# P.V. of all sixteen key tiles accumulated in PSUM, with the next score fill ahead of it on TensorE

## The chip, the cores and the metric

The kernel runs on one core of one Trainium2 chip. A core has a matrix engine (TensorE, PE; its weight loads are shown as PEld), a vector engine (VectorE, DVE), an engine for activation functions (ScalarE, ACT), GpSimd (POOL) and SyncE (SP), which here only issues DMAs. The metric is the device time of one execution in microseconds; lower is better.

## The reference

Four layers run one after the other on x of 2048 rows by 512 columns: attention (A), gated MLP (B), A, B, each with a layernorm ahead and a residual sum behind. The attention has 32 heads of 16 columns that share one K and one V:

```python
q = (x @ wq).reshape(B, S, H, Dh).transpose(0, 2, 1, 3)     # S 2048, H 32, Dh 16
k = x @ wk
v = x @ wv
scores = jnp.einsum('bhqd,bkd->bhqk', q, k) * Dh ** (-0.5)
p = _softmax(scores, axis=-1)
o = jnp.einsum('bhqk,bkd->bhqd', p, v)
return o.transpose(0, 2, 1, 3).reshape(B, S, H * Dh) @ wo
```

Layer B is not touched by the change.

## The kernel before

The kernel writes one list of operations per engine; each engine works its list off in order, and semaphores join them (`K.op`, L53, adds one operation with its waits and its increment). So the order in which `layer_A` calls its helpers is the order on every queue.

**Tiling.** A layer has 4 query chunks (qc) of 512, in each 8 head groups (hg) of 4 heads, and in each of those 16 key tiles (kt) of 128. One triple is a *unit* (L504): 512 units per layer, and 32 *groups* of 16 units. A unit has four *blocks*, one for each head j: the scores of 128 keys by 512 queries, which fill one of PSUM's eight banks.

**Fill** (`emit_fill`, L734): three blocks at a time go into three of banks 0 to 5, each by one matmul that uses 32 rows of the array (L756). Fill i waits until exp i-2 has read those banks. Three blocks make one *iteration* i; there are 683 per layer.

**Exp** (`emit_exp`, L763): one ScalarE instruction reads three banks (128 x 1536) and writes bf16 into three of the twelve slots of `P_ring` (L775). The last one of a layer has two blocks.

**P.V.** (`emit_pv`, L780): four matmuls per unit, one for each head, each on 32 columns of the array, write o transposed into bank 6 (`pv_bank`, L795). A column of ones in `V_aug` gives the denominator of the softmax along with it. Three units fall into every four iterations: in one iteration of four there is none (`iu`, L519).

**Accumulation** (`emit_acc`, L800): DVE copies bank 6 into `acc_sb` at the first key tile (L816), adds bank 6 to it at the next fourteen (L818) and at the last one adds and writes bf16 into `oT_bf` (L820). The next P.V. waits for this read of bank 6 (semaphore `S_acc`, L789).

**Side tasks** (`emit_side_pe`, L535, and `emit_side_dve`, L568): everything else of the layer goes in small tasks, a TensorE part into bank 7 and a DVE part out of it. A task's TensorE part waits for the DVE part of the task before, since there is one side bank. Tasks are: K, V and the transposed x (at the start), the q projections (L489), the transposes of `w_sp` for layer B (L624, layer 0 only, with its DMAs, L611 and L645), at each group's end four transposes of `oT_bf` with a reciprocal and a normalising multiply (`make_fin_task`, L661 to L675), and at each chunk's end two transposing tasks and four projections by `wo` (L699, L717, L722). Urgent tasks may go in every iteration, the others in every second.

**The order of one iteration** (L838 to L846): exp i; P.V. and its accumulation of the units whose blocks are now all there; fill i+2; one side task's TensorE part; one side task's DVE part.

Of the kernel before, what the change touches and what calls it, by code (L numbers as in the profile page):

```python
# [5 lines left out]
FP32 = mybir.dt.float32  # L6
BF16 = mybir.dt.bfloat16
ACTF = mybir.ActivationFunctionType
ALU = mybir.AluOpType
# [95 lines left out]
def bass_interleave_layers__grouped_kv_mqa__mixer_gmlp__prompt_kernel(  # L105
# [16 lines left out]
    NT = S // 128  # L122
    QC = min(512, S)
    assert S % QC == 0
    NQC = S // QC
    NQT = QC // 128
# [4 lines left out]
    K = _B(nc)  # L131
    P = 128
# [16 lines left out]
    S_acc = K.sem()  # L149
# [32 lines left out]
    def pool_memset(ap, val, waits=()):  # L182
# [7 lines left out]
        waits=[(S_pool, v_id0)], inc=S_pool)  # L190
# [4 lines left out]
    with ExitStack() as wst:  # L195
# [23 lines left out]
        def dve_memset(ap, val, waits=()):  # L219
# [8 lines left out]
            waits=[(S_dve, v0), wA], inc=S_dve)  # L228
# [6 lines left out]
            waits=[(S_dve, v0), wA], inc=S_dve)  # L235
# [6 lines left out]
            waits=[(S_dve, v0), wA], inc=S_dve)  # L242
# [91 lines left out]
    def layer_A(layer_idx, x_waits, do_wspt=False):  # L334
# [6 lines left out]
        xn = K.sb([P, NT, D], BF16, lst, name="xnA")  # L341
        qT_pad = K.sb([P, 8, S], BF16, lst, name="qT_pad")
        P_ring = K.sb([P, 12, QC], BF16, lst, name="P_ring")
        acc_sb = K.sb([P, QC], FP32, lst, name="acc_sb")
        oT_bf = K.sb([P, 2, QC], BF16, lst, name="oT_bf")
        o_norm = K.sb([P, NQT, D], BF16, lst, name="o_norm")
        onT = K.sb([P, 2, 4, QC], BF16, lst, name="onT")
# [313 lines left out]
        def make_fin_task(qc, hg, par, acc_val):  # L661
            def pe_fn(e):
                ins = None
                for qt in range(NQT):
                    ins = e.transpose(side_bank16[:, qt * 128:(qt + 1) * 128], oT_bf[:, par, qt * 128:(qt + 1) * 128], ident[:])  # L665
                return ins

            def dve_recip(e):
                src = side_bank16[:, 0:NQT * 128].rearrange("p (qt j r) -> p qt j r", qt=NQT, j=4)[:, :, :, DH]
                return e.reciprocal(rden[:, 0:NQT, :], src)  # L670

            def dve_norm(e):
                src = side_bank16[:, 0:NQT * 128].rearrange("p (qt j r) -> p qt j r", qt=NQT, j=4)[:, :, :, 0:DH]
                dst = o_norm[:, 0:NQT, hg * 64:(hg + 1) * 64].rearrange("p qt (j d) -> p qt j d", d=DH)
                return e.tensor_tensor(dst, src, rden[:, 0:NQT, :, None].to_broadcast([P, NQT, 4, DH]), ALU.mult)  # L675

            task = {
                "pe": pe_fn,
                "pe_waits": [(S_acc, acc_val), (S_pool, v_ident)],
                "dve": [dve_recip, dve_norm],  # L680
                "dve_waits": [],
                "urgent": True,
            }

            def on_pe(v, par=par, grp=qc * 8 + hg):
                fin_pe_val[par] = v
                fin_pe_grp[par] = grp
            task["on_pe_emitted"] = on_pe
            return task

        def make_ont_task(qc, half, par):
            qts = [qt for qt in range(2 * half, min(2 * half + 2, NQT))]

            def pe_fn(e):
                ins = None
                for qi2, qt in enumerate(qts):
                    for c in range(4):
                        slot = qi2 * 4 + c
                        ins = e.transpose(side_bank16[:, slot * 128:(slot + 1) * 128],  # L699
                                          o_norm[:, qt, c * 128:(c + 1) * 128], ident[:])  # L700
                return ins

            def dve_fn(e):
                nq = len(qts)
                dst = onT[:, par, :, qts[0] * 128:(qts[0] + nq) * 128].rearrange("p c (qt q) -> p c qt q", q=128)
                src = side_bank16[:, 0:nq * 4 * 128].rearrange("p (qt c q) -> p c qt q", qt=nq, c=4)
                return e.tensor_copy(dst, src)

            return {"pe": pe_fn, "pe_waits": [(S_pool, v_ident)], "dve": [dve_fn], "dve_waits": [], "urgent": True}

        def make_wo_task(qc, qt, par):
            t = qc * NQT + qt

            def pe_fn(e):
                ins = None
                for c in range(4):
                    ins = e.matmul(side_bank32[:, 0:D], onT[:, par, c, qt * 128:(qt + 1) * 128], wo_r[:, c, :],  # L717
                                   start=(c == 0), stop=(c == 3))
                return ins

            def dve_fn(e):
                return e.tensor_tensor(X[:, t, :], side_bank32[:, 0:D], X[:, t, :], ALU.add)  # L722

            task = {"pe": pe_fn, "pe_waits": [wA], "dve": [dve_fn], "dve_waits": xw_for(x_waits, t), "urgent": True}

            def on_dve(v):
                x_done_vals.append(v)
            task["on_dve_emitted"] = on_dve
            return task
# [33 lines left out]
        def emit_exp(i):  # L763
            blocks = fill_blocks(i)
            n = len(blocks)
            b0 = 3 * (i % 2)
            s0 = (3 * i) % 12
            wl = [(S_fill, fill_base + i + 1)]
            if i >= 4:
                old_blocks = fill_blocks(i - 4)  # L770
                max_u = old_blocks[-1] // 4
                wl.append((S_pv, pv_base + max_u + 1))

            def act_fn(e, n=n, b0=b0, s0=s0):
                return e.activation(P_ring[:, s0:s0 + n, :],  # L775
                                    bank32(b0, n).rearrange("p (k q) -> p k q", k=n)[:, :, 0:QC],
                                    ACTF.Exp, scale=DH ** -0.5)
            K.op("act", act_fn, waits=wl, inc=S_exp)

        def emit_pv(u):  # L780
            qc, hg, kt = units[u]
            kc = kt // CT
            while kc not in V_ready:
                progressed = emit_side_pe()
                progressed = emit_side_dve() or progressed
                assert progressed, "V block task missing"
            wl = [(S_exp, exp_base + iu(u) + 1), V_ready[kc], prologue_done]
            if u >= 1:
                wl.append((S_acc, acc_base + u))  # L789

            def pe_fn(e):
                ins = None
                for j in range(4):
                    slot = (4 * u + j) % 12
                    ins = e.matmul(pv_bank[32 * j:32 * j + 32, 0:QC], V_aug[:, kt, 32 * j:32 * j + 32], P_ring[:, slot, :],  # L795
                                   tile_position=(0, 32 * j), start=True, stop=True)
                return ins
            K.op("pe", pe_fn, waits=wl, inc=S_pv)

        def emit_acc(u):  # L800
            qc, hg, kt = units[u]
            grp = u // NT
            par = grp % 2
            wl = [(S_pv, pv_base + u + 1)]
            if u >= 1:
                wl.append((S_acc, acc_base + u))
            last = (kt == NT - 1)
            if last and grp >= 2:
                while fin_pe_grp[par] != grp - 2:
                    assert emit_side_pe(allow_bg=False), "pending finalize missing"  # L810
                    emit_side_dve()
                wl.append((S_spe, fin_pe_val[par]))
            if NT == 1:
                fn = lambda e: e.tensor_copy(oT_bf[:, par, :], pv_bank[:, 0:QC])
            elif kt == 0:
                fn = lambda e: e.tensor_copy(acc_sb[:], pv_bank[:, 0:QC])  # L816
            elif not last:
                fn = lambda e: e.tensor_tensor(acc_sb[:], pv_bank[:, 0:QC], acc_sb[:], ALU.add)  # L818
            else:
                fn = lambda e: e.tensor_tensor(oT_bf[:, par, :], pv_bank[:, 0:QC], acc_sb[:], ALU.add)  # L820
            v = K.op("dve", fn, waits=wl, inc=S_acc)
            if last:
                side_urgent.append(make_fin_task(qc, hg, par, v))
                if hg == 7:
                    qpar = qc % 2
                    nhalf = (NQT + 1) // 2
                    for half in range(nhalf):
                        side_urgent.append(make_ont_task(qc, half, qpar))
                    for qt in range(NQT):
                        side_urgent.append(make_wo_task(qc, qt, qpar))  # L830

        pending_pv = {}
        for u in range(U):
# [3 lines left out]
            emit_fill(1)  # L837
        for i in range(NI):  # L838
            emit_exp(i)
            for u in pending_pv.get(i, []):  # L840
                emit_pv(u)
                emit_acc(u)
            if i + 2 < NI:
                emit_fill(i + 2)
            emit_side_pe(allow_bg=(i % SIDE_PERIOD == 0))
            emit_side_dve()  # L846
        for i in range(NI, NI + 8):
            for u in pending_pv.get(i, []):
                emit_pv(u)
                emit_acc(u)  # L850
        while side_pending() or side_state["k_dve"] < len(side_emitted):
            progressed = emit_side_pe()
            progressed = emit_side_dve() or progressed
# [258 lines left out]
    v = None  # L1112
# [36 lines left out]
```

## Time and profile before

| | us |
|---|---|
| median of 3 runs | 2634.82 (2631.36 to 2640.33) |
| span of the profiled execution | 2633.1 |
| TensorE busy (PE) | 1897.9 (72%) |
| VectorE busy | 1225.5 (47%) |
| ScalarE busy | 2066.9 (78%) |
| GpSimd busy | 43.9 (2%) |

The profile gives the profiled execution by its span, from the first instruction to the last; there is no other time for it. Busy is the time in which an engine had at least one instruction running; instructions of one engine can overlap, so the number of instructions times their mean duration can be more than the busy time. "Idle before" is the time without any instruction ahead of an instruction, with what ended it. PEclk is the granted clock of TensorE as a share of 2.4 GHz.

### The profile page before, as it was taken

The numbers are of one execution on the slowest core, as the hardware profiler recorded it, in microseconds if no ns is written. First come the engines' busy times: TensorE is split into PE (matmuls) and PEld (weight loads), VectorE is DVE, ScalarE is ACT, GpSimd is POOL, SyncE is SP. The second block draws the span as 40 slices with busy tenths as digits, with TensorE's granted clock in tenths as the row PEclk, the third lists the DMA queues.
The fourth block names the chain that finished last, engine by engine and source line by source line (L and its number), as shares of the span: only waits on it lengthen the run. The fifth ranks groups of instructions, "written<-read, shape, count | busy, mean of one in ns | idle before, by whom it ended". The sixth has DMA issues, their size and how long they took to land.

```text
span 2633.1 us, 29515 instructions
## 1 busy us (share of the span) xinstructions
PE 1897.9 (72%) x11173; PEld 538.9 (20%) x11232; DVE 1225.5 (47%) x2059; ACT 2066.9 (78%) x1639; POOL 43.9 (2%) x95
## 2 busy tenths in 40 slices
PE   2878777777777777468958777777777777764799
PEld 1223111111111111213422111111111111112244
DVE  5565433343334333695366434333433343337933
ACT  1999999999999999181029999999999999973800
POOL 0000000000000000110000000000000000001100
PEclk9996555555555555589979655555655555556899
DMA  3035000000000000201000000000000000001020
GB/s 114 1 88 153 1 1 1 1 1 1 1 1 1 1 1 1 64 1 32 32 1 1 0 1 1 0 1 0 1 1 1 1 0 1 1 1 64 0 68 29
DMA packets 60092, 44.00 MB, mean 17 GB/s; under 512 B 34865, under 2 KB 57265, under 8 KB 59953
## 3 DMA queue, kind: packets, MB, share of 16 engines
q1 hardware_dynamic: 59952, 42.11, 5.4%
q8 instruction: 92, 1.51, 0.2%
q14 instruction: 48, 0.39, 0.0%
HBM read 31.62 MB, written 10.49 MB: 16 GB/s over the span
## 4 chain that ended last, share of the span: by engine, by line
PE 43%; DVE 27%; ACT 20%; issue 8%; POOL 1%; DMA 0%; SPq 0%; another core or an unknown queue 0%; ACTq 0%
PE ps_all L795 20%; ACT P_ring L775 20%; DVE acc_sb L818 13%; PE ps_all L1060 7%; PE ps_all L756 7%; DVE ybuf L951 2%; PE ps_all L1092 2%; PE ps_all L717 2%; DVE ln_stats L277 1%; DVE z2n L972 1%; DVE oT_bf L820 1%; DVE z1c L972 1%; PE ps_all L665 1%; DVE acc_sb L816 1%; PE ps_all L489 1%
## 5 line engine op out<-in xcount | busy, mean ns | idle before, releaser
L775 ACT ACTIVATE P_ring<-ps_all 128x1536 bf16<-128x1536 f32 (+1 forms) x1366 | 1909.5, 1452 | 296.2 <-PE ps_all L756 264.0
L818 DVE TENSOR_TENSOR acc_sb<-ps_all,acc_sb 128x512 f32<-128x512 f32 x896 | 618.1, 690 | 911.2 <-PE ps_all L795 909.8
L795 PE MATMUL ps_all<-P_ring,V_aug 128*32 128x512 bf16 x4096 | 595.9, 569 | 466.8 <-ACT P_ring L775 262.8
L756 PE MATMUL ps_all<-qT_pad,kT_rep 32*128 32x512 bf16 x4096 | 777.7, 568 | 27.1 <-ACT P_ring L775 13.4
L795 PEld LDWEIGHTS ps_all<-P_ring,V_aug 128*32 128x32 bf16 x4096 | 128.6, 100 | 928.3 <-ACT P_ring L775 889.5
L756 PEld LDWEIGHTS ps_all<-qT_pad,kT_rep 32*128 32x128 bf16 x4096 | 141.0, 97 | 580.6 <-issue 416.1
L1060 PE MATMUL ps_all<-wspT,z2n 128*128 128x512 bf16 x878 | 196.8, 383 | 7.7 <-issue 6.8
L942 ACT ACTIVATE ybuf<-ps_all 128x448 f32<-128x448 f32 (+1 forms) x120 | 66.0, 550 | 106.6 <-PE ps_all L904 106.6
L1060 PEld LDWEIGHTS ps_all<-wspT,z2n 128*128 128x128 bf16 x896 | 88.2, 99 | 115.3 <-issue 11.8
L904 PE MATMUL ps_all<-w_in_r,xnTB 128*128 128x448 bf16 x256 | 73.0, 424 | 40.3 <-DVE z2n L972 38.1
L1070 DVE TENSOR_TENSOR gtmp<-ps_all,bsp_bc 128x512 f32<-128x512 f32 x56 | 38.7, 691 | 124.8 <-PE ps_all L1060 124.8
L951 DVE SCALAR_TENSOR_TENSOR ybuf<-ybuf,ps_all 128x448 f32<-128x448 f32 (+1 forms) x120 | 75.3, 628 | 6.4 <-ACT ybuf L942 6.4
L820 DVE TENSOR_TENSOR oT_bf<-ps_all,acc_sb 128x512 bf16<-128x512 f32 x64 | 44.2, 690 | 69.7 <-PE ps_all L795 69.5
L962 ACT ACTIVATE thbuf<-ybuf 128x448 bf16<-128x448 f32 (+1 forms) x120 | 71.2, 594 | 6.7 <-DVE ybuf L951 3.2
L909 PE MATMUL ps_all<-xnTB,w_in_r 128*128 128x512 bf16 x218 | 59.3, 394 | 16.1 <-DVE z1c L972 11.2
L489 PE MATMUL ps_all<-xnTA,wq_pad 128*128 128x512 bf16 x224 | 62.0, 397 | 4.3 <-issue 1.7
L494 DVE CAST qT_pad<-ps_all 128x512 bf16<-128x512 f32 x60 | 41.5, 691 | 50.0 <-PE ps_all L489 50.0
L665 PE MATMUL ps_all<-ident,oT_bf 128*128 128x128 bf16 x256 | 37.2, 296 | 20.2 <-DVE oT_bf L820 20.2
L303 PE MATMUL ps_all<-ident,xnB 128*128 128x128 bf16 x128 | 15.1, 312 | 49.8 <-DVE xnB L292 49.8
L717 PE MATMUL ps_all<-wo_r,onT 128*128 128x512 bf16 x120 | 40.6, 469 | 13.0 <-DVE X L722 6.6
L816 DVE COPY acc_sb<-ps_all 128x512 f32<-128x512 f32 x64 | 43.7, 682 | 9.3 <-PE ps_all L795 9.1
L277 DVE BATCH_NORM_STATS2 ln_stats<-X 128x6 f32<-128x512 bf16 x64 | 42.5, 664 | 0.2
(72 smaller groups left out, 752.2 us busy)
## 6 DMA issues: line engine op xcount, KB each, us to landing
wspT<-wspt_scratch SPq DMA_DIRECT2D x8, 2048.0 KB, 8.3
wsp_stage_21<-in_B_w_sp_dram SPq DMA_DIRECT2D x16, 512.0 KB, 3.9
wspt_scratch<-wspT_tile SPq DMA_DIRECT2D x16, 512.0 KB, 5.0
X<-in_A_x_dram SPq DMA_DIRECT2D x4, 512.0 KB, 5.7
out_dram<-X SPq DMA_DIRECT2D x16, 128.0 KB, 2.9
w_in_r<-in_B_w_in_dram SPq DMA_DIRECT2D x1, 1792.0 KB, 9.6
w_out_r<-in_B_w_out_dram SPq DMA_DIRECT2D x1, 896.0 KB, 10.8
wq_nat<-in_A_wq_dram SPq DMA_DIRECT2D x1, 512.0 KB, 8.0
```

The lines of the kernel that those rows point to most:

```text
L489: ins = e.matmul(side_bank32[:, 0:QC], wq_pad[:, kd, hg, :], xnT[:, kd, qc * QC:(qc + 1) * QC], start=(kd == 0), stop=(kd == KD - 1))
L717: ins = e.matmul(side_bank32[:, 0:D], onT[:, par, c, qt * 128:(qt + 1) * 128], wo_r[:, c, :], start=(c == 0), stop=(c == 3))
L756: ins = e.matmul(bk[:, 0:QC], kT_rep[32 * j:32 * j + 32, kt * 128:(kt + 1) * 128], qT_pad[32 * j:32 * j + 32, hg, qc * QC:(qc + 1) * QC], ...
L775: return e.activation(P_ring[:, s0:s0 + n, :], bank32(b0, n).rearrange("p (k q) -> p k q", k=n)[:, :, 0:QC], ACTF.Exp, scale=DH ** -0.5)
L795: ins = e.matmul(pv_bank[32 * j:32 * j + 32, 0:QC], V_aug[:, kt, 32 * j:32 * j + 32], P_ring[:, slot, :], tile_position=(0, 32 * j), start ...
L816: fn = lambda e: e.tensor_copy(acc_sb[:], pv_bank[:, 0:QC])
L818: fn = lambda e: e.tensor_tensor(acc_sb[:], pv_bank[:, 0:QC], acc_sb[:], ALU.add)
L820: fn = lambda e: e.tensor_tensor(oT_bf[:, par, :], pv_bank[:, 0:QC], acc_sb[:], ALU.add)
L904: ins = e.matmul(bk[:, 0:448], xnT[:, kd, t * 128:(t + 1) * 128], w_in_r[:, kd, FH + h * 448:FH + (h + 1) * 448], start=(kd == 0), stop=(k ...
L951: st["d3"][k] = K.op("dve", lambda e, slot=slot, bk=bk, n=n: e.scalar_tensor_tensor(ybuf[:, slot, 0:n], ybuf[:, slot, 0:n], GELU_C, bk[:, ...
L962: st["a1"][k] = K.op("act", lambda e, slot=slot, n=n: e.activation(thbuf[:, slot, 0:n], ybuf[:, slot, 0:n], ACTF.Tanh), waits=wl, inc=S_act)
L1060: ins = e.matmul(bk[:, 0:TCW], z2n[:, sti, ft * 128:(ft + 1) * 128], wspT[:, wb, sti, :], start=(sti == 0), stop=(sti == NT - 1))
```

## The change

`emit_pv` starts the sum in bank 6 at the first key tile (`start=first`) and leaves it running to the last (`stop=last`), so that TensorE itself adds the sixteen key tiles. `emit_acc` becomes `emit_evac`, which runs once per group: DVE copies bank 6 into `oT_bf` as bf16. A P.V. waits on `S_acc` only where it is the first of a group. `acc_sb` is gone. And fill i+2 now comes ahead of the P.V. of iteration i.

```diff
             wl = [(S_exp, exp_base + iu(u) + 1), V_ready[kc], prologue_done]
-            if u >= 1:
-                wl.append((S_acc, acc_base + u))
+            first = (kt == 0)
+            last = (kt == NT - 1)
+            grp = u // NT
+            if first and grp >= 1:
+                wl.append((S_acc, acc_base + grp))
 
             def pe_fn(e):
                 ins = None
                 for j in range(4):
                     slot = (4 * u + j) % 12
                     ins = e.matmul(pv_bank[32 * j:32 * j + 32, 0:QC], V_aug[:, kt, 32 * j:32 * j + 32], P_ring[:, slot, :],
-                                   tile_position=(0, 32 * j), start=True, stop=True)
+                                   tile_position=(0, 32 * j), start=first, stop=last)
                 return ins
             K.op("pe", pe_fn, waits=wl, inc=S_pv)
-
-        def emit_acc(u):
+            if last:
+                emit_evac(u)
+
+        def emit_evac(u):
             qc, hg, kt = units[u]
             grp = u // NT
             par = grp % 2
             wl = [(S_pv, pv_base + u + 1)]
-            if u >= 1:
-                wl.append((S_acc, acc_base + u))
-            last = (kt == NT - 1)
-            if last and grp >= 2:
+            if grp >= 2:
                 while fin_pe_grp[par] != grp - 2:
                     assert emit_side_pe(allow_bg=False), "pending finalize missing"
                     emit_side_dve()
                 wl.append((S_spe, fin_pe_val[par]))
...
+            v = K.op("dve", lambda e: e.tensor_copy(oT_bf[:, par, :], pv_bank[:, 0:QC]), waits=wl, inc=S_acc)
+            side_urgent.append(make_fin_task(qc, hg, par, v))
...
         for i in range(NI):
             emit_exp(i)
+            if i + 2 < NI:
+                emit_fill(i + 2)
             for u in pending_pv.get(i, []):
                 emit_pv(u)
-                emit_acc(u)
-            if i + 2 < NI:
-                emit_fill(i + 2)
             emit_side_pe(allow_bg=(i % SIDE_PERIOD == 0))
             emit_side_dve()
```

## Rows read from the trace of the kernel before

**Rows 1.** The page: shares of the chain that ended last; the exp's group.
```profile
PE ps_all L795 20%; ACT P_ring L775 20%; DVE acc_sb L818 13%; PE ps_all L1060 7%; PE ps_all L756 7%; DVE ybuf L951 2%; PE ps_all L1092 2%; PE ps_all L717 2%; DVE ln_stats L277 1%; DVE z2n L972 1%; DVE oT_bf L820 1%; DVE z1c L972 1%; PE ps_all L665 1%; DVE acc_sb L816 1%; PE ps_all L489 1%
...
L775 ACT ACTIVATE P_ring<-ps_all 128x1536 bf16<-128x1536 f32 (+1 forms) x1366 | 1909.5, 1452 | 296.2 <-PE ps_all L756 264.0
```

**Rows 2.** Attention by stretch: from:to, length, busy us (x instructions) of each engine, PEclk.
```profile
52.84:91.36 38.52, 31.13 (x280) 13.00 (x283) 22.80 (x38) 35.08 (x26) 0.00 (x0) 0.96 0.00 1
91.36:199.34 107.98, 83.91 (x665) 28.70 (x668) 64.60 (x102) 103.41 (x77) 0.00 (x0) 0.92 0.23 59
199.34:276.39 77.05, 63.13 (x469) 23.81 (x466) 40.00 (x64) 70.93 (x51) 0.00 (x0) 0.61 0.48 124
276.39:1052.88 776.49, 563.72 (x3370) 123.44 (x3373) 300.83 (x465) 744.64 (x531) 0.00 (x0) 0.52 0.00 1
...
1398.86:1487.22 88.36, 67.58 (x479) 19.73 (x482) 49.31 (x79) 85.85 (x63) 0.00 (x0) 0.90 0.00 1
1487.22:2353.97 866.75, 628.49 (x3766) 136.82 (x3769) 335.87 (x519) 834.47 (x595) 0.00 (x0) 0.52 0.00 1
```

**Rows 3.** Timeline, ScalarE, runs of exps: start us, length us, [idle before <-releaser].
```profile
591.02 61.37 ACT L775 ACTIVATE P_ring<-ps_all 128x1536 bf16<-128x1536 f32 x43 [0.50 <-PE ps_all L756]
652.90 30.13 ACT L775 ACTIVATE P_ring<-ps_all 128x1536 bf16<-128x1536 f32 x21 [0.51 <-PE ps_all L756]
683.52 61.38 ACT L775 ACTIVATE P_ring<-ps_all 128x1536 bf16<-128x1536 f32 x43 [0.50 <-PE ps_all L756]
```

**Rows 4.** Timeline inside one run: single exps, then PE, PEld and DVE beside them.
```profile
703.40 1.45 ACT L775 ACTIVATE P_ring<-ps_all 128x1536 bf16<-128x1536 f32 x1
704.91 1.45 ACT L775 ACTIVATE P_ring<-ps_all 128x1536 bf16<-128x1536 f32 x1
706.41 1.45 ACT L775 ACTIVATE P_ring<-ps_all 128x1536 bf16<-128x1536 f32 x1
707.76 1.45 ACT L775 ACTIVATE P_ring<-ps_all 128x1536 bf16<-128x1536 f32 x1
...
703.70 0.62 PE L795 MATMUL ps_all<-P_ring,V_aug 128*32 128x512 bf16 x4 [0.35 <-DVE acc_sb L818]
704.25 0.61 PE L756 MATMUL ps_all<-qT_pad,kT_rep 32*128 32x512 bf16 x3
704.37 0.69 DVE L818 TENSOR_TENSOR acc_sb<-ps_all,acc_sb 128x512 f32<-128x512 f32 x1 [0.81 <-PE ps_all L795]
705.21 0.62 PE L795 MATMUL ps_all<-P_ring,V_aug 128*32 128x512 bf16 x4 [0.34 <-DVE acc_sb L818]
706.41 0.10 PEld L756 LDWEIGHTS ps_all<-qT_pad,kT_rep 32*128 32x128 bf16 x3 [0.56 <-ACT P_ring L775]
```

**Rows 5.** Timeline, single exps in the warm stretch of layer 0.
```profile
103.46 1.45 ACT L775 ACTIVATE P_ring<-ps_all 128x1536 bf16<-128x1536 f32 x1
104.79 1.46 ACT L775 ACTIVATE P_ring<-ps_all 128x1536 bf16<-128x1536 f32 x1
106.12 1.47 ACT L775 ACTIVATE P_ring<-ps_all 128x1536 bf16<-128x1536 f32 x1
```

**Rows 6.** Timeline at a group's end, ahead of the exp at 652.90.
```profile
650.40 0.69 DVE L820 TENSOR_TENSOR oT_bf<-ps_all,acc_sb 128x512 bf16<-128x512 f32 x1 [2.02 <-PE ps_all L795]
...
651.15 0.61 PE L665 MATMUL ps_all<-ident,oT_bf 128*128 128x128 bf16 x4 [0.26 <-DVE oT_bf L820]
...
651.69 0.62 PE L795 MATMUL ps_all<-P_ring,V_aug 128*32 128x512 bf16 x4
...
652.24 0.61 PE L756 MATMUL ps_all<-qT_pad,kT_rep 32*128 32x512 bf16 x3
```

**Rows 7.** Timeline, the exps that begin and end a chunk's end.
```profile
555.22 1.45 ACT L775 ACTIVATE P_ring<-ps_all 128x1536 bf16<-128x1536 f32 x1
...
569.53 1.45 ACT L775 ACTIVATE P_ring<-ps_all 128x1536 bf16<-128x1536 f32 x1
```

**Rows 8.** Timeline, a spatial-weight transposing task and the P.V. behind it.
```profile
215.28 1.03 PE L624 MATMUL ps_all<-ident,wsp_stage_21 128*128 128x128 bf16 x8
...
216.25 0.62 PE L795 MATMUL ps_all<-P_ring,V_aug 128*32 128x512 bf16 x4
```

More of the change, by code (lines that the diff above doesn't have):

```diff
@@ L343, in layer_A @@
         P_ring = K.sb([P, 12, QC], BF16, lst, name="P_ring")
-        acc_sb = K.sb([P, QC], FP32, lst, name="acc_sb")
         oT_bf = K.sb([P, 2, QC], BF16, lst, name="oT_bf")
@@ L812, in emit_acc @@
                 wl.append((S_spe, fin_pe_val[par]))
[L813 to L830, printed above, removed]
+            v = K.op("dve", lambda e: e.tensor_copy(oT_bf[:, par, :], pv_bank[:, 0:QC]), waits=wl, inc=S_acc)
+            side_urgent.append(make_fin_task(qc, hg, par, v))
+            if hg == 7:
+                qpar = qc % 2
+                nhalf = (NQT + 1) // 2
+                for half in range(nhalf):
+                    side_urgent.append(make_ont_task(qc, half, qpar))
+                for qt in range(NQT):
+                    side_urgent.append(make_wo_task(qc, qt, qpar))
         pending_pv = {}
@@ L849, in layer_A @@
                 emit_pv(u)
-                emit_acc(u)
         while side_pending() or side_state["k_dve"] < len(side_emitted):
```

## The prediction

> **What bounds the kernel now.** I read the page's chain and the ScalarE line first, then a table of busy time by stretch, then single instructions. The chain [rows 1] gives P.V. 20%, the accumulating add 13% and exp 20% of the span, while the exp line says ScalarE is 1909.5 us busy with 296.2 us idle, most of which lies ahead of the two attention layers. So ScalarE looks like a bound with hardly a gap, and the chain contradicts it. The stretches [rows 2] show attention of layer 0 from 52.84 to 1052.88 us and of layer 2 from 1360.34 to 2353.97: 1993.7 us for 2 x 683 exps. Two stretches, 276.39 to 1052.88 and 1487.22 to 2353.97, hold 531 and 595 exps at a granted clock of 0.52, that is at TensorE's 1.2 GHz level but for short bursts. I call them the cold stretches; the rest of attention, but for 199.34 to 276.39, is near 2.4 GHz.
>
> In a cold stretch ScalarE shows runs of 43 and 21 exps with a gap of 0.50 or 0.51 us between them [rows 3]; three head groups (64 exps) take 683.52 - 591.02 = 92.50 us, 1.445 us per exp. The single instructions inside a "gapless" run tell more [rows 4]: exp starts at 703.40, 704.91, 706.41, 707.76, steps of 1.51, 1.50 and 1.35, with one duration, 1.45. Consecutive exps overlap, so a step of 1.50 holds a hidden wait of 0.15 or more that no idle column counts. In the warm stretch the steps are 1.33 [rows 5].
>
> What makes 1.51 is beside it in [rows 4]: P.V. issues at 703.70, its add starts on DVE at 704.37 and takes 0.69, the next P.V. issues at 705.21. That loop, 0.67 + 0.69 + 0.15 = 1.51 us, is longer than an exp, and the score fill that feeds the next exp stands behind the P.V. on TensorE's queue: P.V. 703.70, fill 704.25, exp 704.91. So in cold stretches the bound is the round P.V. -> add -> P.V., handed on to ScalarE through the fill. Three units follow in four exps, and the fourth step is slack; this mixes 1.51 and 1.35 into about 1.43.
>
> **The change, part by part.** (1) Removed: per head group fifteen adds or copies of 0.69 on DVE, 960 in all with 64 groups. On DVE itself they cost nothing, it is under half busy. What they cost is the round of 1.51. With accumulation in PSUM the next P.V. waits only for its exp.
>
> (2) Moved: the fill goes ahead of the P.V. on TensorE, so exp to fill to exp no longer holds a P.V. By [rows 4], an exp from 704.91 lasts to 706.36 and the fill's weights load at 706.41, 0.05 later; a fill issued at 704.25 lets its exp start at 704.91, 0.66 later. So the scores are there 0.05 + 0.66 = 0.71 us after the exp before the last, while ScalarE is inside an exp of about 1.33. TensorE's own work per exp, cold, is one fill and one P.V. With P.V. to fill measured at 0.55 and fill to P.V., which the trace does not show, between the same 0.55 and the fill's 0.62, it is 1.10 to 1.17, under 1.33. I take 0.55, the nearest switch between the two shapes. Both cover ends hold: ScalarE is next to be late. Per exp I take 1.335: the steps of 1.33 of [rows 5], and one of 1.35 after each stall. Bounds are 1.33 and the 1.36 that cold steps reach.
> Cold stretches so: 531 x 1.335 = 708.9 and 595 x 1.335 = 794.3 us, before stalls.
>
> (3) The end of a head group. Before [rows 6]: evacuating add 650.40, transposes of oT_bf 651.15 (0.75 later), P.V. 651.69, fill 652.24, exp 652.90, after a gap of 0.51; in one group of three the next iteration has no P.V. and nothing is late. After the change, counted from the end of an exp: fill 0.05, last P.V. 0.60, evacuation (a copy, same size as the add, 0.69) 1.27, transposes 2.02, next fill 2.56, its exp 3.22. Without a stall that exp would start 2 x 1.335 after an exp that began about 0.15 before the count: 2.52. So the stall is about 0.7 (I take 0.69), and at every group end, since the moved P.V. puts a fill ahead of the evacuation and the transposes wait for it in front of the next fill. This is the part that gets worse. Queued behind that waiting transpose are the next fill and P.V.; ScalarE waits for them. The new wait of a group's first P.V. on the evacuation costs nothing: the transposes ahead of it on the queue have waited for the same copy. The wait for the transposes of two groups ago is as before. Cold stretches hold 24 and 27 group ends that have exps behind them; three of each also end a query chunk. 21 x 0.69 = 14.5 and 24 x 0.69 = 16.6.
>
> (4) The three chunk ends per layer queue a transposing and projecting task in each of seven iterations. Before, seven steps of exp starts [rows 7] from 555.22 take 14.31, 4.97 over 7 x 1.335. Following the new order through the same tasks gives 4 to 5: each side task still waits on the single side bank, between a P.V. and the next fill. I take 4.9, so 14.7 per layer. No gain here.
>
> (5) The other stretches [rows 2]. Start, 25 exps in 38.52, once in each layer (the second from 1360.34): 5.1 over 25 x 1.335, mostly the K and V tasks' round through DVE; DVE has no add in between, I take 1.5 back each (bounds 0 and 5.1). 91.36 to 199.34 and 1398.86 to 1487.22, warm: 6.5 and 4.3 over; I take 4.5 and 3 (bounds 0 and all). 199.34 to 276.39, with two spatial-weight transposes per four exps, is TensorE-bound when cold: 4 fills + 3 P.V. at 0.55 and two tasks of 0.97 [rows 8] make 5.79 per four exps, 73.8 for 51: 3.3 back (bounds 0 and 9). SP's DMAs of that stretch hang on the same tasks, in the same order; TensorE is passed by no other queue, POOL's and SP's are not touched. Layer B is untouched.
>
> **Sum.** Layer 0 cold: 708.9 + 14.5 + 14.7 = 738.1 against 776.5: 38.4. Layer 2 cold: 794.3 + 16.6 + 14.7 = 825.6 against 866.8: 41.2. Others: 3 + 7.5 + 3.3 = 13.8. Together 93.4. From the profiled span of 2633.1 that leaves 2539.7; the median of the runs, 2634.82, lies 1.7 above the span, so 2541 us, 3.6% less.
>
> Against this stands the Trainium skill, ScalarE: Activation LUTs, section What ACT_TABLE_LOAD costs: an activation with immediate operands takes 186 ns + 0.833 ns per element, and neighbours overlap by 93 ns. For 1536 elements that is an estimate of 1.47 and a step of 1.37; the duration agrees with 1.45 here, the step does not with 1.33 [rows 5]. By the skill's step the sum would be 0.038 x 1126 = 43 us worse, 2584; by the rows it is 2541.
>
> **The rivals.**
> *A: ScalarE's own step is 1.36, not 1.335.* For it: exps that follow a hidden wait step 1.35. Against: 1.33 in [rows 5], where scores are early, as they would be now. Price 0.025 x 1126 = 28: 2569. Chance 0.10. The Trainium skill's figure above lies on this side, and further out.
> *B: TensorE, busier in less time, stays at 2.4 GHz.* For it: it did so in the warm stretches. Against: there it has dense side work, and with fills and P.V. alone it fell to 0.5 each time; the mix grows denser by only 8%. The group-end stalls would go (45 x 0.69 = 31), of the chunk ends some 20, of the mixed stretch 5: 2485. Chance 0.10.
> *C, the slower side: the cold cadence isn't the add's round, only the group ends change.* If ScalarE or cold TensorE itself makes 1.43, nothing is gained per exp, while the group end goes from 0.51 at two of three to 0.69 at all: 45 x 0.69 - 30 x 0.51 = +16, 2651 us. For it: no idle shows on ScalarE within runs. Against: the hidden wait of [rows 4], exactly the round's 1.51. It decides once the gain per exp is under (0.69 - 0.34) / 21.3 = 0.016 us, of 0.09 expected. Chance 0.05.
> *D: the waits stay,* because the first P.V. of a group or the evacuation is held by something else: no change, 2635. Chance 0.03.
>
> **How the numbers follow.** The forecast has 0.72. Its upper bounds: fill to P.V. at 0.62 (45 x 0.07 = 3), 1.36 per exp (28), nothing in (5) (14), chunk ends 1 us worse each (6): 2592. Lower: 1.33 per exp (6), all of (5) (16), chunk ends halved (15), group stalls 0.5 (9): 2495. The range is 2497 to 2592, which takes in A and stops short of B. What this kernel's measurement can tell from no change is about 0.3%, 8 us. Faster: forecast, A and B, 0.92; same, D, 0.03; slower, C, 0.05.
>
> **What would show it.** Right: exp starts 1.33 to 1.35 apart inside a group; no wait of P.V. on DVE but at group ends; a gap near 0.7 on ScalarE in each of 45 cold group ends, ahead of a fill; DVE busy about 660 us less (960 x 0.69). Wrong: steps still at 1.43 or more (C), a granted clock near 1 in cold stretches (B), gaps of over 1 us at group ends, or fills that wait for a P.V. before them.

## The result, and the profile after

| | before | after |
|---|---|---|
| median, us | 2633.33 (2631.36 to 2640.33, 4 runs) | 2544.03 (2543.25 to 2547.78, 4 runs) |
| ratio, 95% interval | | 0.9657 [0.9639, 0.9675] |
| span of the profiled execution, us | 2633.1 | 2541.3 |
| DVE busy, us | 1225.5 | 577.0 |
| ScalarE busy, us | 2066.9 | 2003.9 |

The change makes the kernel 3.4% faster, 91.8 us by the two spans. The forecast was 2541 us for the median and 2539.7 for the span.

The page of the kernel after: the chain's shares by line, the group of the exp, and that of the evacuation (count, busy us, mean ns, then idle us ahead and its releaser). They answer to [rows 1].

```profile
ACT P_ring L774 29%; PE ps_all L1050 8%; PE ps_all L755 4%; DVE ybuf L941 2%; PE ps_all L797 2%; PE ps_all L1082 2%; DVE oT_bf L814 2%; PE ps_all L716 2%; DVE ln_stats L277 2%; PE ps_all L664 1%; DVE z2n L962 1%; DVE z1c L962 1%; PE ps_all L303 1%; DVE st_59 L967 1%; DVE st_37 L967 1%
...
L774 ACT ACTIVATE P_ring<-ps_all 128x1536 bf16<-128x1536 f32 (+1 forms) x1366 | 1846.6, 1560 | 268.3 <-PE ps_all L755 267.8
...
L814 DVE CAST oT_bf<-ps_all 128x512 bf16<-128x512 f32 x64 | 44.3, 692 | 1422.0 <-PE ps_all L797 1421.8
```

P.V. has gone from 20% of the chain to 2%, the add is gone, the exp leads. The mean exp has become *longer*, 1560 ns for 1452, and yet there are more of them per microsecond: they overlap more. So the mean duration of this instruction says little about its pace; the start times do.

Attention by stretch in the kernel after, cut at the same exps as [rows 2] (from:to, length, then busy us and count for PE, PEld, DVE, ACT, POOL, and PEclk):

```profile
52.94:89.56 36.62, 29.38 (x277) 12.59 (x280) 12.66 (x21) 34.43 (x25) 0.00 (x0) 1.00 0.00 1
89.56:262.92 173.36, 135.65 (x1135) 48.89 (x1137) 47.13 (x75) 171.58 (x127) 0.00 (x0) 0.88 0.36 92
262.92:1002.59 739.67, 562.13 (x3374) 117.01 (x3373) 45.58 (x91) 717.42 (x531) 0.00 (x0) 0.52 0.00 1
...
1309.54:1347.47 37.93, 30.69 (x277) 13.01 (x280) 12.66 (x21) 34.42 (x25) 0.00 (x0) 0.96 0.00 1
1347.47:1433.75 86.28, 67.61 (x483) 19.48 (x485) 20.90 (x34) 84.99 (x63) 0.00 (x0) 0.89 0.00 1
1433.75:2262.71 828.96, 629.55 (x3770) 130.45 (x3769) 49.71 (x100) 803.71 (x595) 0.00 (x0) 0.52 0.00 1
```

The two cold stretches, 531 and 595 exps, give 776.49 - 739.67 = 36.8 and 866.75 - 828.96 = 37.8 us. The stretch from 89.56 to 262.92 answers to two of before, 91.36 to 276.39, and gives 11.7. The clock in the cold stretches is 0.52 as before.

Inside a cold stretch, ScalarE's timeline: two runs, and three single exps of the second of them, the last of which ends it (start us, length us, and in brackets the idle time before). They answer to [rows 3] and [rows 4].

```profile
355.18 28.32 ACT L774 ACTIVATE P_ring<-ps_all 128x1536 bf16<-128x1536 f32 x21 [0.53 <-PE ps_all L755]
384.02 28.32 ACT L774 ACTIVATE P_ring<-ps_all 128x1536 bf16<-128x1536 f32 x21 [0.53 <-PE ps_all L755]
...
400.00 1.59 ACT L774 ACTIVATE P_ring<-ps_all 128x1536 bf16<-128x1536 f32 x1
401.33 1.61 ACT L774 ACTIVATE P_ring<-ps_all 128x1536 bf16<-128x1536 f32 x1
410.64 1.70 ACT L774 ACTIVATE P_ring<-ps_all 128x1536 bf16<-128x1536 f32 x1
```

Exps start every 1.33 us, with one step of 1.35 behind each stall; the steps of 1.51 are gone. Over a run of 21 that is (410.64 - 384.02) / 20 = 1.331 per exp. A run now ends at every group end (21 or 22 exps); before there were runs of 43 as well. From 355.18 to 384.02 is 28.84 us for 21 exps, 0.89 more than 21 x 1.331. That is the stall. The idle column shows only 0.53 of it, because the exp ahead of a stall lasts 1.70, 0.37 more than a step. Along a run each exp lasts a little longer than the one before, from 1.45 to 1.70, so the ends of a run's exps are (28.32 - 1.45) / 20 = 1.343 apart while the starts are 1.331 apart.

Where the 0.89 comes from, on TensorE and DVE around 412 us; this answers to [rows 6].

```profile
409.70 0.61 PE L755 MATMUL ps_all<-qT_pad,kT_rep 32*128 32x512 bf16 x3 [0.18 <-ACT P_ring L774]
410.24 0.62 PE L797 MATMUL ps_all<-P_ring,V_aug 128*32 128x512 bf16 x4
410.92 0.69 DVE L814 CAST oT_bf<-ps_all 128x512 bf16<-128x512 f32 x1 [26.73 <-PE ps_all L797]
411.66 0.61 PE L664 MATMUL ps_all<-ident,oT_bf 128*128 128x128 bf16 x4 [0.80 <-DVE oT_bf L814]
412.20 1.03 PE L755 MATMUL ps_all<-qT_pad,kT_rep 32*128 32x512 bf16 x6
412.86 1.45 ACT L774 ACTIVATE P_ring<-ps_all 128x1536 bf16<-128x1536 f32 x1 [0.53 <-PE ps_all L755]
```

Fill, last P.V., evacuation, transposes, next fill, exp: each waits for the one before or stands behind it on TensorE's queue, and from the first fill to the exp it is 3.16 us. TensorE stands still for 0.80 us ahead of the transposes while the exp after the next has no scores yet.

### The profile page after: what moved, and what is told of

Its sections match the earlier page's. It is cut to its first block, busy times and chain, and to the rows that moved or that the text cites. A ratio compares the mean times of both kernels' runs of the same rounds, so it can differ in the third digit from the quotient of the medians.

```text
span 2541.3 us, 26575 instructions
## 1 busy us (share of the span) xinstructions
PE 1881.8 (74%) x11173; PEld 521.4 (21%) x11232; DVE 577.0 (23%) x1099; ACT 2003.9 (79%) x1639; POOL 43.9 (2%) x95
## 4 chain that ended last, share of the span: by engine, by line
issue 34%; ACT 29%; PE 22%; DVE 14%; POOL 1%; DMA 0%; SPq 0%; another core or an unknown queue 0%; ACTq 0%
ACT P_ring L774 29%; PE ps_all L1050 8%; PE ps_all L755 4%; DVE ybuf L941 2%; PE ps_all L797 2%; PE ps_all L1082 2%; DVE oT_bf L814 2%; PE ps_all L716 2%; DVE ln_stats L277 2%; PE ps_all L664 1%; DVE z2n L962 1%; DVE z1c L962 1%; PE ps_all L303 1%; DVE st_59 L967 1%; DVE st_37 L967 1%
## 5 line engine op out<-in xcount | busy, mean ns | idle before, releaser
L774 ACT ACTIVATE P_ring<-ps_all 128x1536 bf16<-128x1536 f32 (+1 forms) x1366 | 1846.6, 1560 | 268.3 <-PE ps_all L755 267.8
L814 DVE CAST oT_bf<-ps_all 128x512 bf16<-128x512 f32 x64 | 44.3, 692 | 1422.0 <-PE ps_all L797 1421.8
L797 PEld LDWEIGHTS ps_all<-P_ring,V_aug 128*32 128x32 bf16 x4096 | 112.6, 100 | 415.8 <-issue 411.7
L894 PEld LDWEIGHTS ps_all<-w_in_r,xnTB 128*128 128x128 bf16 x256 | 23.2, 109 | 89.5 <-DVE z2n L962 67.9
```

The lines of the kernel that those rows point to most:

```text
L774: return e.activation(P_ring[:, s0:s0 + n, :], bank32(b0, n).rearrange("p (k q) -> p k q", k=n)[:, :, 0:QC], ACTF.Exp, scale=DH ** -0.5)
L814: v = K.op("dve", lambda e: e.tensor_copy(oT_bf[:, par, :], pv_bank[:, 0:QC]), waits=wl, inc=S_acc)
L894: ins = e.matmul(bk[:, 0:448], xnT[:, kd, t * 128:(t + 1) * 128], w_in_r[:, kd, FH + h * 448:FH + (h + 1) * 448], start=(kd == 0), stop=(k ...
```

## The experiments

Theory: the cold cadence was the round P.V. - add - P.V., felt by ScalarE because a fill stood behind each P.V.; and the group end of the changed kernel is the chain just shown. All times below are medians of four runs, beside seven of the kernel before on the same chip (medians 2635.0 and 2634.2 on two chips).

| kernel | us | ratio to before, 95% interval |
|---|---|---|
| accumulation alone, old order | 2552.8 | 0.969 [0.9674, 0.9706] |
| order alone, adds kept | 2550.8 | 0.9684 [0.967, 0.9699] |
| changed, closing transposes later | 2503.0 | 0.9504 [0.949, 0.9518] |
| changed, evacuation twice | 2594.5 | 0.9848 [0.9834, 0.9863] |
| changed, every fill twice | 2651.5 | 1.0067 [1.0052, 1.0082] |
| order alone, closing transposes later | 2508.2 | 0.9523 [0.9508, 0.9537] |
| changed, all closing tasks later | 2496.0 | 0.9475 [0.9459, 0.9491] |

### The two edits one at a time

Accumulation alone puts the old order back into the changed kernel:

```diff
             emit_exp(i)
+            for u in pending_pv.get(i, []):
+                emit_pv(u)
             if i + 2 < NI:
                 emit_fill(i + 2)
-            for u in pending_pv.get(i, []):
-                emit_pv(u)
```

> The changed kernel with the old order on TensorE: P.V. accumulates in PSUM, but each iteration's P.V. stands ahead of the next fill again. Theory (the round P.V. - add - P.V. of 1.51 us made the cadence, and either edit alone breaks it): fill ready 0.05 + 0.55 + 0.66 = 1.26 us after an exp's end, so two exps take 1.45 + 1.26 = 2.71, a step of at most 1.355 against 1.333; 1126 cold exps x about 0.018 = +20 us; group ends lose less (last P.V. 0.55 earlier than in the changed kernel: stall about 0.67 at two of three, 0.13 at the third, against 0.86 at all: -17 us). Sum 2546 us, between 2535 and 2565. Rival (each of the two edits carries about half of the gain): about 2590. Rival (the order is what counts): near 2633.

Measured 2552.8 us. Its ScalarE timeline, two runs and two single exps, TensorE between those two, and attention of layer 0 by stretch:

```profile
898.59 28.50 ACT L774 ACTIVATE P_ring<-ps_all 128x1536 bf16<-128x1536 f32 x21 [0.51 <-PE ps_all L755]
927.60 58.34 ACT L774 ACTIVATE P_ring<-ps_all 128x1536 bf16<-128x1536 f32 x43 [0.50 <-PE ps_all L755]
...
406.10 1.45 ACT L774 ACTIVATE P_ring<-ps_all 128x1536 bf16<-128x1536 f32 x1
407.45 1.45 ACT L774 ACTIVATE P_ring<-ps_all 128x1536 bf16<-128x1536 f32 x1
...
406.24 0.62 PE L797 MATMUL ps_all<-P_ring,V_aug 128*32 128x512 bf16 x4 [0.18 <-ACT P_ring L774]
406.79 0.61 PE L755 MATMUL ps_all<-qT_pad,kT_rep 32*128 32x512 bf16 x3
...
53.63:271.78 218.15, 176.13 (x1423) 64.49 (x1421) 59.74 (x95) 207.18 (x152) 0.00 (x0) 0.85 0.29 73
271.78:1011.81 740.03, 564.15 (x3373) 116.69 (x3369) 45.43 (x90) 721.83 (x531) 0.00 (x0) 0.52 0.00 1
```

The step is 1.35 (over the long run (58.34 - 1.45) / 42 = 1.3545, the 1.355 of the expectation), and the pattern of 21 and 43 is back: one group end in three costs nothing. P.V. now waits for the exp, not for DVE. The cold stretch is as long as with the whole change, 740.03 against 739.67 us: what the longer step loses, the group ends give back. Of the 9 us between the two kernels 8.2 lie ahead of it, 218.15 us against 36.62 + 173.36 = 209.98.

Order alone moves the fill in the kernel before and leaves every add:

```diff
             emit_exp(i)
+            if i + 2 < NI:
+                emit_fill(i + 2)
             for u in pending_pv.get(i, []):
                 emit_pv(u)
                 emit_acc(u)
-            if i + 2 < NI:
-                emit_fill(i + 2)
```

> The kernel before with the fill ahead of P.V.; each P.V. is still copied or added by DVE, and the next P.V. still waits for that. Theory (the round alone fits: three rounds of 1.51 = 4.53 us are under four exps of 1.333 = 5.33 us; it hurt only because a fill stood behind it): cadence 1.333 inside groups, group ends like the changed kernel's or up to 0.3 us worse because the last P.V. lags behind; 2543 to 2575 us, I take 2552. Rival (the round itself is the bound, TensorE's order is beside the point): 2633. Rival (half and half): about 2590.

Measured 2550.8 us. ScalarE's runs, then TensorE and DVE inside one, and attention of layer 0 by stretch:

```profile
417.80 29.66 ACT L775 ACTIVATE P_ring<-ps_all 128x1536 bf16<-128x1536 f32 x22 [0.67 <-PE ps_all L756]
447.98 28.32 ACT L775 ACTIVATE P_ring<-ps_all 128x1536 bf16<-128x1536 f32 x21 [0.52 <-PE ps_all L756]
...
408.39 0.62 PE L795 MATMUL ps_all<-P_ring,V_aug 128*32 128x512 bf16 x4
409.06 0.69 DVE L818 TENSOR_TENSOR acc_sb<-ps_all,acc_sb 128x512 f32<-128x512 f32 x1 [0.72 <-PE ps_all L795]
409.12 0.61 PE L756 MATMUL ps_all<-qT_pad,kT_rep 32*128 32x512 bf16 x3
409.81 0.62 PE L795 MATMUL ps_all<-P_ring,V_aug 128*32 128x512 bf16 x4
...
53.22:267.85 214.63, 173.13 (x1419) 63.92 (x1417) 130.74 (x200) 206.55 (x153) 0.00 (x0) 0.86 0.29 74
267.85:1007.86 740.01, 576.34 (x3377) 116.35 (x3373) 304.35 (x466) 717.45 (x531) 0.00 (x0) 0.52 0.00 1
```

Runs of 21 exps are 28.32 us long, as with the whole change, although each P.V. still waits for its add. The round goes on (408.39 to 409.81 is 1.42; a fill now runs beside the add) and costs nothing, because the fill at 409.12 no longer waits for it. Inside the cold stretches only the group ends show it: 0.52 and 0.67 in these rows, where the last P.V. lags. The two cold stretches as a whole are as long as the changed kernel's (740.01 and 828.84 us against 739.67 and 828.96). Of the 7 us between the two kernels 4.7 lie ahead of the first cold stretch, where TensorE's granted clock was 0.66 in the last 51 exps (193.63 to 267.85), against 0.79 in the changed kernel (193.21 to 262.92).

So the two edits aren't two halves: either takes nearly the whole gain, 82 and 84 us of 91, and all of it in the cold stretches. Both rivals, half and half (2590) and one edit alone counting (2633), are out.

### The group end

The evacuation is done twice:

```diff
-            v = K.op("dve", lambda e: e.tensor_copy(oT_bf[:, par, :], pv_bank[:, 0:QC]), waits=wl, inc=S_acc)
+            v0 = K.op("dve", lambda e: e.tensor_copy(oT_bf[:, par, :], pv_bank[:, 0:QC]), waits=wl, inc=S_dloc)
+            v = K.op("dve", lambda e: e.tensor_copy(oT_bf[:, par, :], pv_bank[:, 0:QC]), waits=[(S_dloc, v0)], inc=S_acc)
```

> The changed kernel with each group's evacuation copy made twice, one after the other. Theory (evacuation lies on the path at every group end): +0.69 to 0.75 us at each of 64 group ends, a few of the warm ones partly hidden: +40 to +48 us, 2583 to 2591 us, with gaps of about 1.25 us on ScalarE in place of 0.53. Rival (the gap is TensorE's own work and the copy is hidden): 2543.

Measured 2594.5 us. One group end of its trace:

```profile
425.88 0.69 DVE L814 CAST oT_bf<-ps_all 128x512 bf16<-128x512 f32 x1 [26.73 <-PE ps_all L797]
426.60 0.69 DVE L815 CAST oT_bf<-ps_all 128x512 bf16<-128x512 f32 x1
427.35 0.61 PE L664 MATMUL ps_all<-ident,oT_bf 128*128 128x128 bf16 x4 [1.53 <-DVE oT_bf L815]
...
428.55 29.66 ACT L774 ACTIVATE P_ring<-ps_all 128x1536 bf16<-128x1536 f32 x22 [1.25 <-PE ps_all L755]
```

The gap goes from 0.53 to 1.25, by the 0.72 from one copy to the next, and it does so at each of the 45 cold group ends: the copy is on the path there. The kernel loses 50 us, above the 40 to 48 expected. The two cold stretches hold 34.8 of them (757.97 and 845.41 us). Another 12.1 lie ahead of the first (222.12 us against 209.98), where the clock was lower too, 0.64 in the last 51 exps (199.77 to 274.75) against 0.79; what the copy costs there by itself is not shown.

Then the other way: a list of its own, `side_late`, for the closing tasks. The four transposes (marked `fin`) are taken from it only in an iteration without a P.V. (`i % 4 == 0`), the tasks of a chunk's end in any. Of the edit, the lines that do this:

```diff
-            side_urgent.append(make_fin_task(qc, hg, par, v))
+            late = side_late
+            late.append(make_fin_task(qc, hg, par, v))
...
-            emit_side_pe(allow_bg=(i % SIDE_PERIOD == 0))
+            emit_side_pe(allow_bg=(i % SIDE_PERIOD == 0), allow_late=(i % 4 == 0 or not (side_late and side_late[0].get('fin'))))
```

> The changed kernel, but the four transposes that close a head group are held back to the next iteration without a P.V. (one in four), so TensorE does not stand waiting for the evacuation ahead of a fill. Theory (the stall at group ends is evacuation -> transposes -> fill, about 0.86 us over the step at each of some 45 cold group ends): those gaps go, 2543 - 39 = 2504 us; the six chunk ends lose about the same as now or one stall less. Rival (the transposes themselves, 0.55 us of TensorE, cost the time wherever they stand): 2520 to 2543.

Measured 2503.0 us. One run of ScalarE and a single exp of it, and TensorE and DVE at a group end inside it:

```profile
303.97 225.97 ACT L778 ACTIVATE P_ring<-ps_all 128x1536 bf16<-128x1536 f32 x168 [0.37 <-PE ps_all L759]
405.54 1.97 ACT L778 ACTIVATE P_ring<-ps_all 128x1536 bf16<-128x1536 f32 x1
...
405.42 0.62 PE L801 MATMUL ps_all<-P_ring,V_aug 128*32 128x512 bf16 x4
406.09 0.69 DVE L818 CAST oT_bf<-ps_all 128x512 bf16<-128x512 f32 x1 [24.83 <-PE ps_all L801]
406.23 0.61 PE L759 MATMUL ps_all<-qT_pad,kT_rep 32*128 32x512 bf16 x3 [0.19 <-ACT P_ring L778]
406.84 0.61 PE L667 MATMUL ps_all<-ident,oT_bf 128*128 128x128 bf16 x4
407.57 0.61 PE L759 MATMUL ps_all<-qT_pad,kT_rep 32*128 32x512 bf16 x3
```

168 exps without a gap, from one chunk end to the next. The fill at 406.23 runs under the evacuation, the same transposes come behind it, and the next fill is on time. So the gap was the wait, not the transposes' own time. The changed kernel had left 41 us lying here, 37 of them in the cold stretches (722.12 and 809.40 us). In so long a run the exps settle at 1.97 us each and start (225.97 - 1.97) / 167 = 1.341 apart: the steps of 1.33 are those of short runs, behind a stall.

Does DVE's relief count for anything once nothing stands behind it? The same hold on the transposes, in the kernel with the new order and all its adds (its edit is the order and the holding back shown above, together):

> The kernel before with the fill ahead of P.V. and the closing transposes held back to an iteration without a P.V., but with DVE's add per unit kept (no accumulation in PSUM). Theory (the add's round costs nothing once no fill stands behind it): within 10 us of the same kernel with accumulation, 2503 to 2515 us. Rival (accumulation is worth something by itself, through DVE or the round): 2525 or more.

Measured 2508.2 us, 5.2 more than with accumulation. The run between two chunk ends is as long as its counterpart just shown:

```profile
306.51 225.98 ACT L779 ACTIVATE P_ring<-ps_all 128x1536 bf16<-128x1536 f32 x168 [0.37 <-PE ps_all L760]
```

DVE is busy for 304.91 us of this cold stretch, against 46.12 with accumulation, and the run is 0.01 us longer. The whole cold stretches are equal too (722.49 and 809.34 us against 722.12 and 809.40). What accumulation is worth beside the order is at most these 5 us, and they lie elsewhere; the intervals of the two ratios overlap (0.9508 to 0.9537 and 0.949 to 0.9518), so it isn't shown that it is worth anything here.

### All closing tasks held back

The condition is `allow_late=(i % 4 == 0)`, for the transposing and projecting tasks of a chunk's end too.

> The changed kernel with all closing tasks of groups and chunks (transposes and projections too) only in iterations without a P.V. Theory (what is left at chunk ends is side tasks and P.V. in one iteration): transposing tasks cost nothing there, each of four projections 0.6 to 0.7 us at 1.2 GHz, so some 1 us less at each of six chunk ends than with the closing transposes alone held back: about 2498 us. Rival (no difference, the projections cost the same wherever they stand, as the clock no longer rises): 2503.

Measured 2496.0 us, the fastest of all these kernels, 48 us under the changed one. The cold stretches are 12.7 us shorter than with the transposes alone held back (716.36 and 802.47 us), the rest of the execution 5.8 longer. At the first cold chunk end two gaps of 0.38 us are left, where the kernel with late transposes has five of 0.37 to 0.42:

```profile
311.47 16.44 ACT L777 ACTIVATE P_ring<-ps_all 128x1536 bf16<-128x1536 f32 x12 [0.38 <-PE ps_all L758]
328.29 215.04 ACT L777 ACTIVATE P_ring<-ps_all 128x1536 bf16<-128x1536 f32 x160 [0.38 <-PE ps_all L758]
```

### What TensorE's clock is worth

Each fill issues its three matmuls twice (the second ones write the same scores again):

```diff
-                for b in blocks:
+                for b in blocks + blocks:
```

> The changed kernel with the three matmuls of every fill issued twice (the second ones write the same scores over the first), to tell what TensorE's clock is worth. If the clock stays at 1.2 GHz in the cold stretches: per four exps 4 x (0.42 + 0.55) + 3 x 0.55 = 5.53 us of TensorE against 5.33 of ScalarE, TensorE becomes the bound: +56 us, and group ends about 0.4 us worse each, about 2615 us. If the busier TensorE is granted 2.4 GHz there (rival B of the prediction): ScalarE is the bound with 1.333 per exp, the 45 cold group stalls and part of the chunk ends go: about 2490 us, granted clock near 1 in attention.

Measured 2651.5 us: the clock did not rise in the cold stretches. A part of one (columns as for the stretches above) and two runs of ScalarE:

```profile
600.00:800.00 200.00, 193.83 (x1252) 32.09 (x1248) 8.25 (x18) 189.54 (x138) 0.00 (x0) 0.50 0.00 1
...
425.58 30.93 ACT L774 ACTIVATE P_ring<-ps_all 128x1536 bf16<-128x1536 f32 x22 [1.48 <-PE ps_all L755]
457.71 29.68 ACT L774 ACTIVATE P_ring<-ps_all 128x1536 bf16<-128x1536 f32 x21 [1.20 <-PE ps_all L755]
```

TensorE is busy for 193.83 of 200 us and is granted 0.50. Rival B of the prediction, out already by the 0.52 of the changed kernel, does not come back with more work for TensorE in this mix of matmuls. The size was 36 us beyond the cold estimate of 2615. An exp takes (30.93 - 1.45) / 21 = 1.404, where 5.53 / 4 = 1.3825 was expected: 1126 x 0.021 = 24 us. The group ends are some 6 us more: from 425.58 to 457.71 it is 32.13 - 22 x 1.404 = 1.24 over the step, and 1.5 where the gap is 1.48, where 0.86 + 0.4 = 1.26 was expected. The few us that are left are not accounted for.

The Trainium skill, TensorE: Matmul & The Clock Gate, section Loop structure matters more than you think, has matmuls that follow each other closely keep the array at its full clock. By that rule this kernel would have come near the 2490 us of the expectation's second case; the row above, at 97% busy and 1.2 GHz, does not agree with it. Ahead of the cold stretch, where side tasks stand among the same doubled fills, the clock was 1.00 (92.03 to 195.70) and 0.90 (195.70 to 266.70); which difference between the stretches matters is not shown.

## Why the prediction was right

**The bound.** Right. The hidden waits, steps of 1.51 inside runs that the profile shows without a gap, were the reading on which the forecast hung; that they were the round of P.V. and add, felt through the fill, is shown by the two single edits, each of which takes away one link.

**Part 2, the pace.** 1.335 per exp was forecast, 1.331 was measured, and 1.341 once no stall is left in between. Rival A (1.36) is out; it is nearly what accumulation alone gives. Fill to P.V., which no row of before showed, is 410.24 - 409.70 = 0.54; 0.55 was taken.

**Part 3, the group end.** The mechanism held at every group end, step by step: 3.22 us from an exp's end to the late exp was forecast, and by the rows it is 0.05 + 3.16. The term was mis-sized: 0.69 was forecast, 0.89 measured. The step that failed is the sentence that the exp underway began 0.15 before the count. That is so for exps of 1.45. At a run's end they last 1.7 at a step of 1.33: the exp underway began at 409.31 (1.33 ahead of the one at 410.64), and the count begins at 409.65, 0.05 ahead of the fill. So it began 0.34 before, and the late exp misses its turn by that much more. 45 x 0.20 = 9 us too little stall, against 1126 x 0.004 = 4.5 us of pace. The sign that was given, a gap near 0.7 on ScalarE, did not come either: the gap is 0.53, since a gap and a stall aren't the same where exps overlap.

**Part 4, chunk ends.** 4.9 was forecast for each of six, and no gain. One of them, from its first late exp to the first of the next run in the kernel after, answers to [rows 7]:

```profile
530.91 1.45 ACT L774 ACTIVATE P_ring<-ps_all 128x1536 bf16<-128x1536 f32 x1 [0.53 <-PE ps_all L755]
...
542.11 20.25 ACT L774 ACTIVATE P_ring<-ps_all 128x1536 bf16<-128x1536 f32 x15 [0.37 <-PE ps_all L755]
```

11.20 for six steps is 3.2 over 6 x 1.331, with the 0.89 ahead of 530.91 4.1. The first chunk end, read the same way, is 5.3; all six together are 30.3, 5.0 each.

**Part 5, the other stretches.** 13.8 was forecast; 1.9 + 0.6 (start of the two layers), 11.7 (91.36 to 276.39 before, 7.8 forecast) and 2.1 (3 forecast) make 16.3. The mixed stretch was taken as TensorE-bound at 1.2 GHz. But the clock of its 51 exps rose from 0.61 (199.34 to 276.39) to 0.79 (193.21 to 262.92), and they took 69.71 us where 73.8 was forecast. The prediction had such a rise only in its rival B; why the clock rose here is not shown.

**Sum.** Cold stretches 739.67 and 828.96 against 738.1 and 825.6 forecast, 4.9 us worse; the others 2.5 better; layer B about 1 better. Forecast 2539.7 for the span, measured 2541.3. That the two are so close is in part luck: the group ends were priced too low, the pace and the other stretches too high, and the errors cancel. Rival B is out by the 0.52 of the cold stretches, rival C (2651, slower) and D by the time, and C's mechanism by the steps of 1.33. DVE's busy time fell by 648.5 us, where about 660 was forecast. The prediction's lower bounds add up to 2495; the 2497 of its range is a slip and changes nothing.

What the prediction did not see is that either edit alone would have done: it priced both as one. It had the numbers: three rounds of 1.51 fit under four exps of 1.333, so the order alone would have been enough.

## What to carry to other kernels

Read the pace of a pipelined engine from start times, not from idle columns or mean durations: where instructions overlap, a late start shows as little or no idle (a step of 1.51 with exps of 1.45 leaves 0.06, which the timeline here does not even print). When an engine's queue holds work for the bottleneck behind work that waits for a slower loop, putting the bottleneck's work first can be worth as much as removing the loop. And look at what the reorder does at the seams: the same order that freed the steady state made every group end late, and moving one small task to an iteration with room gave another 41 us.

## What the runs showed of the hardware

Exps of the same size lasted from 1.45 us (after a stall) to 1.70 (at the end of a run of 21) in the changed kernel, with starts 1.33 apart: the overlap of one exp with the next grows from 0.10 to 0.37. In the run of 168 exps of the kernel with late transposes they settle at 1.97, 0.63 more than the step of 1.341. So in these two kernels the length of an exp tells where it stands in its run, not how much work it does. The Trainium skill, ScalarE: Activation LUTs, section What ACT_TABLE_LOAD costs, gives an overlap of 93 ns. An estimate by it has 1126 exps of 1.45 us at steps of 1.36 and the kernel some 29 us slower, as in rival A; the first step behind a stall (1.35) agrees with it, the others show more overlap and a shorter step.

TensorE at 97% busy stayed at 0.50 of its clock over 200 us of 32-row fills and 32-column P.V. At chunk ends, where full-size transposes and projections stand among them, it rose for a few us in the kernels before (0.98 from 565 to 570 us) and after (1.00 from 535 to 540 us). Why it stays down in the one and rises in the other was not tried.
